# Attention, SoLU layer and Sinkhorn experts in one kernel: the first layer's input weights placed over the attention's memory, and the experts' first operands made beside the last units of the second matmul

## The chip, the cores and the metric

The kernel runs on one core of one Trainium2 chip. The metric is the device time of one execution in microseconds (us), lower is better. The program has five engines that work at once: TensorE (PE, matmuls), VectorE (DVE), ScalarE (ACT), GpSimd (POOL) and SyncE (SP, which here only issues DMAs). Each runs its own instructions in the order in which the program lists them.

## The reference, cut to what matters

```python
def reference(...):                       # q, k, v: (2, 8, 768, 64); 1536 tokens of 512 values in all
    # 1. attention with 4 sinks and a window of 128 keys
    scores = where(is_sink | in_window, q @ k.T / 8, -1e9)
    x = (softmax(scores) @ v)             # -> (1536, 512)
    # 2. SoLU layer
    h = x @ w_in                          # (1536, 1024)
    solu = h * softmax(h)
    ln = (solu - mean) / sqrt(var + 1e-6) * g_ln
    x = ln @ w_out                        # (1536, 512), called x2 below
    # 3. eight experts, weighed by a Sinkhorn matrix P (1536, 8) made from x @ w_gate in eight rounds
    for e in range(8):
        out += P[:, e:e+1] * (maximum(x @ w1[e], 0) @ w2[e])   # w1[e]: (512, 1024), w2[e]: (1024, 512)
```

## The kernel before, in words

Every matmul operand is split into a rounded part and a remainder ("hi" and "lo"), and a product is three matmuls, hi·hi, hi·lo and lo·hi (`mm3`, L82 to L88, whose three lines L83, L85 and L87 carry most matmuls of the trace).

*Attention and layer 2, tile by tile.* The 1536 tokens are 12 tiles of 128. A loop over slots s (eight heads a tile, 96 slots, and some more to drain) emits, for each slot, the scores of one head (`sc`), the softmax (`soft_exp`), transposes of the softmax of a pair of heads (`a_tr`, L494), the products with v (`av`, L522), and for each finished tile its normalisation and transposition (`x_tr`). Tile t then gets an "h unit" (`h_unit`): 24 matmuls into the PSUM tile hp, and behind it a chain of small steps: maximum (L235, DVE), exp (L238, ACT), product (L241, DVE), square (L249, ACT), power (L252, POOL), normalisation (L256, DVE), gains (L257, POOL), then transposes (L268, PE) and their split into `lt` (L67 ACT, L68 DVE). Each two tiles an "x2 unit" (`x2_unit`, 96 matmuls in two halves of 48, PSUM tile x2p) multiplies by w_out and puts the result into the four blocks x2f of 384 tokens. A half is copied out of PSUM by ACT (L310), or, where it straddles two blocks (x2 units 1 and 4), by ACT (L312) and DVE (L313). Units are numbered from 0: the last ones are h unit 11 and x2 units 4 (tiles 8 and 9) and 5 (tiles 10 and 11).

*The order.* Matmuls of h and x2 units wait in a queue, from which each slot takes 1.0 to 1.3 us worth (`bulk`). The small steps are emitted under `beside()`. A planner then orders each engine's instructions: of those that its own timing model calls ready, the one that stands first in the program. `tc.high_priority(offset=n)` counts an instruction as n places earlier; `beside()` has offset 0, the steps of an h unit's chain 60.

*Experts.* w1 is read in slices of 128 columns of each half (`load_w1`), combined by four sums (L684 to L687, POOL) into seven products' operands, and split by POOL (L76 rounds, L80 subtracts); w2 likewise without sums. The token side has seven operands for each half of the tokens, `build_x(n)`: sums and differences of x2f blocks (t1 to t4, L649) and "puts" (L644 ACT rounds, L645 DVE subtracts). `run` goes through 64 units (slice s, token half n): `first` is seven products of six matmuls (L716), with ReLU by ACT (L728) and its remainder by DVE (L729); `second`, of the unit before, is 36 matmuls and six accumulations. Slices 0 and 1 are made in `begin` (which follows the last x2 unit in the program) and `go_on`; build_x(0) stands in `begin`, build_x(1) as a whole ahead of unit 1. The logits and the Sinkhorn rounds are stepped beside the units (`step_side`).

*Memory.* Tiles live in pools that are opened and closed like a stack, from the left or the right. A tile laid over old ones waits until those that it overlaps have been read for the last time. Before, w_in and w_out share one pool that is closed after the last x2 unit; x0, wf (raw slices and temporaries) and w1a lie over the attention's pool; w1b, w2p and x1 over w_in and w_out.

## Time and profile before

| what | value |
|---|---|
| three runs, median | 1362.09 us (1361.94 to 1362.51) |
| profiled execution, its own time | 1362.57 us |
| its span, first to last instruction | 1360.5 us |
| PE busy | 1317.5 us, 97% |
| DVE, ACT, POOL busy | 708.2, 373.4, 541.9 us |
| mean granted PE clock | 0.982 of full speed |
| HBM traffic over the span | 41 GB/s |

All times in a trace are from the start of the span. The granted clock is given as a share of full speed: 1.00 is 2.4 GHz, 0.50 is 1.2 GHz. The attention and layer 2 take about the first 338 us, the experts the rest. Matmuls are pipelined, so their listed durations overlap.

### The profile page before, as it was taken

Reading aid. Unit: us, or ns where it says so; the run is one execution under the profiler, and the core shown is the slowest. Engines: PE = TensorE matmul, PEld = TensorE weight load, DVE = VectorE, ACT = ScalarE, POOL = GpSimd, SP = SyncE. Lnnn points to the kernel's source line nnn. Section 1 sums busy time; section 2 is a strip of 40 time slices with the busy share of each in tenths; the row PEclk is TensorE's granted clock in tenths of the full one; section 3 lists DMA queues with packets and bytes.
Section 4 is the critical chain, followed back from the end, with each engine's and each line's share of the span. In section 5 each row is a group of like instructions: output and inputs, shape, how many; then the busy total and the mean of one; then the engine's idle time right before and its main releaser. Section 6 shows DMA issues by size and latency. Waiting matters only on the chain.

```text
span 1360.5 us, 17867 instructions
## 1 busy us (share of the span) xinstructions
PE 1317.5 (97%) x6993; PEld 1171.5 (86%) x6993; DVE 708.2 (52%) x1352; ACT 373.4 (27%) x837; POOL 541.9 (40%) x560
## 2 busy tenths in 40 slices
PE   6799999987999999999999999999999999999998
PEld 5678888886789898989999999989999989999986
DVE  7976554544657454444444444544444544444544
ACT  5666454632422111111111111111111111111111
POOL 7862111243733643444333334444343333334410
PEclk9779999997999999999999999999999999999999
DMA  7411211001101111101111111111111001101102
GB/s 219 136 50 32 47 32 24 9 17 31 47 20 43 32 32 43 36 31 47 32 31 32 32 31 31 32 33 45 32 39 40 32 32 31 32 31 32 32 1 96
DMA packets 86287, 56.38 MB, mean 41 GB/s; under 512 B 41520, under 2 KB 74288, under 8 KB 86192
## 3 DMA queue, kind: packets, MB, share of 16 engines
q1 hardware_dynamic: 86192, 55.13, 13.8%
q8 instruction: 57, 0.93, 0.3%
q14 instruction: 38, 0.31, 0.1%
HBM read 51.97 MB, written 3.15 MB: 41 GB/s over the span
## 4 chain that ended last, share of the span: by engine, by line
PE 89%; DVE 4%; ACT 1%; issue 1%; POOL 0%; DVEq 0%; POOLq 0%; ACTq 0%
PE pb L716 15%; PE p L87 13%; PE p L85 13%; PE p L83 13%; PE pa L716 10%; PE pd L716 5%; PE pz L716 5%; PE av L522 2%; PE x2p L83 2%; PE x2p L85 2%; PE x2p L87 1%; PE hp L87 1%; PE hp L83 1%; PE hp L85 1%; DVE x L645 1%; PE trp L494 1%
## 5 line engine op out<-in xcount | busy, mean ns | idle before, releaser
L783 DVE SCALAR_TENSOR_TENSOR xa<-p,pr,xa 128x512 f32<-128x512 f32 x348 | 250.7, 748 | 207.0 <-PE p L87 207.0
L85 PE MATMUL p<-w,h 128*128 128x512 f32 x768 | 301.3, 392 | 0.0
L83 PE MATMUL p<-w,h 128*128 128x512 f32 x768 | 300.1, 391 | 0.5 <-DVE xa L783 0.5
L87 PE MATMUL p<-w,h 128*128 128x512 f32 x768 | 282.0, 394 | 2.1 <-DVE h L729 2.1
L716 PE MATMUL pb<-x,w 128*128 128x384 f32 x1152 | 234.0, 338 | 0.0
L76 POOL TENSOR_SCALAR w<-wf 128x1792 fp32r<-128x1792 f32 x32 | 54.3, 1697 | 437.2 <-PE pb L716 437.0
L716 PEld LDWEIGHTS pb<-x,w 128*128 128x128 f32 x1152 | 206.0, 188 | 5.7
L87 PEld LDWEIGHTS p<-w,h 128*128 128x128 f32 x768 | 143.6, 188 | 28.7 <-DVE h L729 2.5
L716 PE MATMUL pa<-x,w 128*128 128x384 f32 x768 | 167.1, 340 | 0.2 <-DVE h L729 0.2
L83 PEld LDWEIGHTS p<-w,h 128*128 128x128 f32 x768 | 144.2, 188 | 25.4 <-issue 0.9
L85 PEld LDWEIGHTS p<-w,h 128*128 128x128 f32 x768 | 144.2, 188 | 21.5
L728 ACT ACTIVATE h<-pz 128x384 fp32r<-128x384 f32 x64 | 31.4, 491 | 449.1 <-DVE pz L750 449.1
L716 PEld LDWEIGHTS pa<-x,w 128*128 128x128 f32 x768 | 139.2, 189 | 13.8 <-DVE h L729 0.5
L80 POOL TENSOR_TENSOR w<-wf,w 128x512 fp32r<-128x512 f32 (+1 forms) x128 | 148.3, 1191 | 2.6
L729 DVE SCALAR_TENSOR_TENSOR h<-pb,h 128x384 fp32r<-128x384 f32 x64 | 35.6, 557 | 159.5 <-ACT h L728 159.5
L80 POOL TENSOR_TENSOR w<-wr,w 128x512 fp32r<-128x512 f32 x64 | 83.7, 1330 | 0.2
L728 ACT ACTIVATE h<-pb 128x384 fp32r<-128x384 f32 x64 | 31.5, 492 | 179.1 <-PE pb L716 179.1
L716 PE MATMUL pz<-x,w 128*128 128x384 f32 x384 | 78.0, 338 | 0.0
L716 PE MATMUL pd<-x,w 128*128 128x384 f32 x384 | 77.9, 337 | 0.0
L750 DVE TENSOR_TENSOR pz<-pb,z 128x384 f32<-128x384 f32 x64 | 36.3, 566 | 76.6 <-PE pb L716 76.6
L716 PEld LDWEIGHTS pz<-x,w 128*128 128x128 f32 x384 | 69.2, 188 | 5.3
L83 PE MATMUL x2p<-lt,w 128*128 128x256 f32 x192 | 58.1, 303 | 10.1 <-DVE xa L313 8.9
(203 smaller groups left out, 1899.8 us busy)
## 6 DMA issues: line engine op xcount, KB each, us to landing
wf<-in_moe_w_dram SPq DMA_DIRECT2D x128, 128.0 KB, 2.3
wr<-in_moe_w_dram SPq DMA_DIRECT2D x32, 512.0 KB, 3.5
raw<-in_moe_w_in_dram SPq DMA_DIRECT2D x8, 512.0 KB, 5.9
raw<-in_moe_w_out_dram SPq DMA_DIRECT2D x8, 512.0 KB, 3.6
qk<-in_q_dram SPq DMA_DIRECT2D x12, 256.0 KB, 2.9
qk<-in_k_dram SPq DMA_DIRECT2D x12, 256.0 KB, 2.7
v<-in_v_dram SPq DMA_DIRECT2D x12, 256.0 KB, 2.8
out_dram<-xa SPq DMA_DIRECT2D x12, 256.0 KB, 3.5
```

The source lines that it names most:

```text
L76: nc.gpsimd.tensor_scalar(hi, src, 1.0, 0.0, ALU.mult, ALU.add)
L80: nc.gpsimd.tensor_tensor(lo[:, cs], src[:, cs], f32(hi[:, cs]), ALU.subtract)
L83: nc.tensor.matmul(ps, lhsT=lh, rhs=rh, start=start, stop=False)
L85: nc.tensor.matmul(ps, lhsT=lh, rhs=rl, start=False, stop=False)
L87: nc.tensor.matmul(ps, lhsT=ll, rhs=rh, start=False, stop=stop)
L494: nc.tensor.transpose(ps[:, hh, z], a[:, o:o + P], ident)
L522: nc.tensor.matmul(self.av_ps[:, h], lhsT=at[:, hh, z], rhs=self.raw["v", tv][:, h], start=h == 0 and n == 0, stop=h == H - 1 and n == len ...
L716: nc.tensor.matmul(ps, lhsT=a, rhs=b, start=start and kk == 0 and z == 0, stop=kk == 1 and z == 2, skip_group_check=True,)
L728: nc.scalar.activation(out=h[j][:, f, 0], in_=ps, func=ACTF.Relu)
L729: nc.vector.scalar_tensor_tensor(out=h[j][:, f, 1], in0=ps, scalar=0.0, in1=f32(h[j][:, f, 0]), op0=ALU.max, op1=ALU.subtract)
L750: nc.vector.tensor_tensor(out=pz, in0=pb, in1=z, op=ALU.add)
L783: nc.vector.scalar_tensor_tensor(out=acc, in0=ps, scalar=self.pr[:, t, e:e + 1], in1=acc, op0=ALU.mult, op1=ALU.add)
```

## The change

w_in gets a pool of its own in the attention's stack, so that it is released with the attention; w_out keeps its own. The experts' pools for raw slices (wfr), temporaries (wf), w2 (w2p) and both w1 buffers (w1a, w1b) open when h unit 11 has been emitted, over the attention and w_in. `build_x` makes seven tiles rather than one with seven parts, each put and difference in two halves, as a generator; `begin` is a generator too and is advanced two steps a slot beside x2 units 4 and 5; it now also splits slices 0 and 1 of w1 and w2. build_x(1) is advanced two steps at a time, twelve times over units 0 and 1. From slot 94 on `beside()` has offset 200. The attention's PSUM banks are released at slot 100, and give h unit 11 its own hp and the last x2 units a second x2p. x2's straddling halves are copied by ACT alone.

```diff
-    def w_slot():
-        n = w_count[0] % 8
-        w_count[0] += 1
-        return wpool.tile([P, 2, F], F32R, name=f"w{n}", tag=f"w{n}")
+    def w_slot(which, n):
+        return wpools[which].tile([P, 2, F], F32R, name=f"w_{which}{n}", tag=f"w_{which}{n}")
...
-    def x2_unit(p, pp):
+    def x2_unit(p, pp, tags=("mm", "mm")):
...
-            ps = pp["mm"].tile([P, 2, 2 * P], F32, name="x2p", tag="mm")
+            ps = pp[tags[d2]].tile([P, 2, 2 * P], F32, name="x2p", tag=tags[d2])
...
-                nc.vector.tensor_copy(x2f[t // 3 + 1][:, ds, 0:P], ps[:, :, P:])
+                nc.scalar.activation(out=x2f[t // 3 + 1][:, ds, 0:P], in_=ps[:, :, P:], func=ACTF.Copy)
...
         def open_early(self, stack):
+            self.wfr = pool(stack, "wfr", side="right")
+            self.wf = pool(stack, "wf", side="right")
+            self.w2p = pool(stack, "w2p", side="right")
+            w1b = pool(stack, "w1b", side="right")
             self.xp = [pool(stack, "x0", side="right")]
-            self.wf = pool(stack, "wf", side="right")
-            self.w1p = [pool(stack, "w1a", side="right")]
+            self.w1p = [pool(stack, "w1a", side="right"), w1b]
...
         def build_x(self, n, tp):
-            x = self.x[n] = self.xp[n].tile([P, 7, 2, 2, NX], F32R, name=f"x{n}")
+            x = self.x[n] = [None] * 7
+            for k in (self.X11, self.T3, self.T1, self.T2, self.X22, self.T4, self.X21):
+                x[k] = self.xp[n].tile([P, 2, 2, NX], F32R, name=f"x{n}_{k}", tag=f"x{n}_{k}")
...
             def put(k, src):
-                nc.scalar.activation(out=x[:, k, 0], in_=src, func=ACTF.Copy)
-                nc.vector.tensor_tensor(out=x[:, k, 1], in0=src, in1=f32(x[:, k, 0]), op=ALU.subtract)
+                for a in range(2):
+                    nc.scalar.activation(out=x[k][:, 0, a], in_=src[:, a], func=ACTF.Copy)
+                    nc.vector.tensor_tensor(
+                        out=x[k][:, 1, a], in0=src[:, a], in1=f32(x[k][:, 0, a]), op=ALU.subtract
+                    )
+                    yield
+            def minus(e, t, a, b):
+                for z in range(2):
+                    e.tensor_tensor(out=t[:, z], in0=a[:, z], in1=b[:, z], op=ALU.subtract)
+                    yield
+            t3, t1 = tp(0), tp(1)
+            yield from minus(nc.gpsimd, t3, b22, b12)
+            yield from put(self.X11, b11)
+            yield from minus(nc.vector, t1, b12, b11)
+            yield from put(self.T3, t3)
+            yield from put(self.X21, b21)
...
-            r = self.raw["1", s] = self.wf.tile([P, 8, 2, P], F32, name="wf", tag="wf")
+            r = self.raw["1", s] = self.wfr.tile([P, 8, 2, P], F32, name="wf", tag="wf")
...
+            build = self.build_x(1, lambda z: self.temp(("tt", "t1")[z]))
             for u, (s, n) in enumerate(units):
-                if u == 1:
-                    self.build_x(1, lambda z: self.temp(("tt", "h1")[z]))
-                if u < 2:
-                    step_side()
-                    step_side()
...
-                for _ in range(6):
+                for z in range(6):
                     next(a, None)
-                    if u > 1:
+                    if u > 1 or z in (1, 2) and not u:
                         step_side()
                     next(b, None)
+                    if u < 2:
+                        next(build, None)
+                        next(build, None)
...
         def begin(self):
-            self.build_x(0, lambda z: self.temp(("tt", "wr")[z]))
             self.load_w1(0)
+            build = self.build_x(0, lambda z: self.temp(("tt", "t1")[z]))
+            for _ in range(4):
+                next(build)
+                yield
             self.split_w1(0)
             self.load_w1(1)
-            self.load_w2(0)
-
-        def go_on(self):
-            for s in range(2):
-                self.split_w2(s)
-                self.load_w2(s + 1)
+            for z, _ in enumerate(build):
+                yield
+                if z == 5:
+                    self.load_w2(0)
+                    self.split_w2(0)
+                    self.load_w2(1)
             self.split_w1(1)
             self.load_w1(2)
+            yield
+            self.split_w2(1)
+            self.load_w2(2)
...
-            return tc.high_priority(offset=0)
+            return tc.high_priority(offset=0 if s < NS - 2 else 200)
...
-                    queue.insert(0, (s + 1, h_unit(tt, fast.x.pop(tt), pp, later, tr_q)))
+                    if tt == T - 1:
+                        psum_a.close()
+                        for nm in ("h", "mm"):
+                            pp[nm + "2"] = pool(psum_b, f"ps_{nm}2", space=PS)
+                    queue.insert(0, (s + 1, h_unit(tt, fast.x.pop(tt), pp, later, tr_q, "h2" if tt == T - 1 else "h")))
...
-            if att_open and s > NS + 6 and not queue:
-                att_open = False
+            if begin is None and s > LX + NS - H and not queue:
                 att.close()
                 ex.open_early(stack)
-                psum_a.close()
-                queue.append((s, x2_unit(T // 2 - 2, pp)))
-                queue.append((s + 10, x2_unit(T // 2 - 1, pp)))
-        ex.begin()
+                queue.append((s, x2_unit(T // 2 - 2, pp, ("mm2", "mm"))))
+                queue.append((s + 10, x2_unit(T // 2 - 1, pp, ("mm", "mm2"))))
+                begin = ex.begin()
+            if begin:
+                next(begin, None)
+                next(begin, None)
```

## Rows read from the trace of the kernel before

**Rows 1.** The page's heading: the span of the profiled execution.

```profile
span 1360.5 us, 17867 instructions
```

**Rows 2.** Windows, PE: stretch, its length, PE busy (matmuls), granted clock, DMA share, GB/s.

```profile
302.30:311.40 9.10, 0.26 (x3) 0.76 0.20 58
311.40:317.20 5.80, 5.78 (x27) 0.50 0.00 0
317.20:319.90 2.70, 2.70 (x23) 0.99 0.00 0
...
350.84:355.30 4.46, 4.46 (x16) 0.62 0.03 8
```

**Rows 3.** Timeline, PE: start, us, line, tiles; in brackets idle time before it, releaser.

```profile
311.42 0.58 PE L83 MATMUL x2p<-lt,w 128*128 128x256 f32 x1 [8.86 <-DVE xa L313]
...
322.43 1.09 PE L268 MATMUL trp<-ident,u 128*128 128x128 f32 x8 [2.47 <-POOL u L257]
...
350.84 0.50 PE L87 MATMUL p<-w,h 128*128 128x512 f32 x1 [2.12 <-DVE h L729]
```

**Rows 4.** Timelines of DVE and POOL, 301 to 325 us: tile 11's chain and what stands between.

```profile
301.13 1.23 DVE L235 TENSOR_REDUCE st<-hp 128x1 f32<-128x1024 f32 x1 [7.83 <-PE hp L87]
...
303.28 5.35 DVE L645 TENSOR_TENSOR x<-xa,x 128x768 fp32r<-128x768 f32 x3
...
309.75 1.21 DVE L241 CUSTOM_DVE_ANT_0 u<-hp,u 128x1024 f32<-128x1024 f32 x1
...
310.96 0.41 DVE L313 COPY xa<-x2p 128x256 f32<-128x256 f32 x1
...
323.75 1.29 DVE L68 TENSOR_TENSOR lt<-trp,lt 128x512 fp32r<-128x512 f32 x2 [2.92 <-ACT lt L67]
...
319.45 2.92 POOL L257 TENSOR_TENSOR u<-u,gains 128x1024 f32<-128x1024 f32 x1 [0.69 <-DVE u L256]
```

**Rows 5.** Timelines of DVE and POOL: first and last step of tile 10's chain.

```profile
283.10 1.22 DVE L235 TENSOR_REDUCE st<-hp 128x1 f32<-128x1024 f32 x1 [0.17 <-PE hp L87]
...
292.16 2.39 POOL L257 TENSOR_TENSOR u<-u,gains 128x1024 f32<-128x1024 f32 x1 [1.21 <-DVE u L256]
```

**Rows 6.** Timeline, ACT and PE: tile 11 from its last softmax to its h unit.

```profile
273.99 0.19 ACT L467 ACTIVATION_READ_ACCUMULATOR a<-a 128x1 f32 x1
...
280.85 0.27 PE L494 MATMUL trp<-ident,a 128*128 128x128 f32 x1
...
285.88 1.00 PE L522 MATMUL av<-v,at 128*128 128x64 f32 x8
...
294.85 0.39 PE L83 MATMUL hp<-w,xt 128*128 128x512 f32 x1
```

**Rows 7.** Timelines of SP and POOL: the first load, sums, rounding and subtraction of slices.

```profile
286.81 22.93 SPq L675 DMA_DIRECT2D wf<-in_moe_w_dram  x8
...
294.51 1.84 POOL L649 TENSOR_TENSOR tt<-xa 128x768 f32<-128x768 f32 x1
296.31 0.74 POOL L685 TENSOR_TENSOR wf<-wf 128x256 f32<-128x256 f32 x1
...
299.47 1.70 POOL L76 TENSOR_SCALAR w<-wf 128x1792 fp32r<-128x1792 f32 x1
301.25 6.56 POOL L80 TENSOR_TENSOR w<-wf,w 128x512 fp32r<-128x512 f32 x4
...
338.40 1.05 POOL L76 TENSOR_SCALAR w<-wr 128x1024 fp32r<-128x1024 f32 x1 [14.54 <-PE x2p L87]
...
394.08 4.49 POOL L80 TENSOR_TENSOR w<-wf,w 128x512 fp32r<-128x512 f32 x4
```

**Rows 8.** The chain that ended last: the same product 52 units apart (start, us, what).

```profile
518.33 1.06 PE pb L716 x6
...
1331.87 1.06 PE pb L716 x6
```

**Rows 9.** Timeline, DVE: a put alone, and three of build_x(1).

```profile
319.23 0.95 DVE L645 TENSOR_TENSOR x<-wr,x 128x768 fp32r<-128x768 f32 x1
...
341.84 6.54 DVE L645 TENSOR_TENSOR x<-xa,x 128x768 fp32r<-128x768 f32 x3
```

More of the change, by code (lines that the diff above doesn't have):

```diff
@@ L217, in drain, with h_unit @@
                 self.slot += 1
-    def h_unit(t, xt, pp, later, tr_q):
-        hp = pp["h"].tile([P, F], F32, name="hp", tag="h")
+    def h_unit(t, xt, pp, later, tr_q, tag="h"):
+        hp = pp[tag].tile([P, F], F32, name="hp", tag=tag)
         for kk in range(KD):
@@ L630, in open_rest @@
             self.xp.append(pool(stack, "x1"))
-            self.w1p.append(pool(stack, "w1b"))
-            self.w2p = pool(stack, "w2p")
             self.hp = pool(stack, "hp")
@@ L643, in put @@
             def put(k, src):
-                nc.scalar.activation(out=x[:, k, 0], in_=src, func=ACTF.Copy)
-                nc.vector.tensor_tensor(out=x[:, k, 1], in0=src, in1=f32(x[:, k, 0]), op=ALU.subtract)
-            def minus(e, z, a, b):
-                t = tp(z)
-                e.tensor_tensor(out=t, in0=a, in1=b, op=ALU.subtract)
-                return t
-            t3 = minus(nc.gpsimd, 0, b22, b12)
-            t1 = minus(nc.vector, 1, b12, b11)
-            put(self.X11, b11)
-            put(self.T3, t3)
-            put(self.X21, b21)
-            t2 = minus(nc.vector, 0, b22, t1)
-            put(self.T1, t1)
-            t4 = minus(nc.gpsimd, 1, b21, t2)
-            put(self.T2, t2)
-            put(self.T4, t4)
-            put(self.X22, b22)
+                for a in range(2):
[14 more added lines that the diff above has]
+            yield from put(self.X21, b21)
+            t2 = tp(0)
+            yield from minus(nc.vector, t2, b22, t1)
+            yield from put(self.T1, t1)
+            yield from put(self.T2, t2)
+            t4 = tp(1)
+            yield from minus(nc.gpsimd, t4, b21, t2)
+            yield from put(self.X22, b22)
+            yield from put(self.T4, t4)
         def temp(self, tag):
-            if tag == "h1":
-                return f32(self.hp.tile([P, 2, 2, NX], F32R, name="h1", tag="h1", bufs=2))[:, 0]
             return self.wf.tile([P, 2, NX], F32, name=tag, tag=tag)
@@ L793, in x_parts @@
             if b % 2 == 0:
-                return x[:, self.X11], x[:, self.X21]
+                return x[self.X11], x[self.X21]
             t = self.hp.tile([P, 2, 2, NX], F32R, name="h0", tag="h0", bufs=2)
@@ L1150, in general_path @@
         ex.open_early(stack)
-        ex.begin()
+        for _ in ex.begin():
+            pass
         ex.open_rest(stack)
```

28 lines of the change are left out of this document (15 added, 13 removed).

## The prediction

> **What bounds the kernel now.** I read the page first: the span is 1360.5 us [rows 1], and TensorE (PE) is busy almost all of it, so only stretches in which PE stands still or runs at the low clock can be won. The profiled execution took 1362.57 us, 2.07 us more than its span and 0.48 us more than the median of the runs shown.
>
> The PE windows of the stretch that the change touches come next [rows 2]. Until 302.3 PE is full. From 302.3 to 311.4 it works 0.26 of 9.10 us; then 27 matmuls take 5.80 us at a granted clock of 0.50 (1.2 GHz), where 23 matmuls of the same x2 unit take 2.70 us at 0.99, 0.117 us each. The reader is to see a long gap and, right behind it, half speed. From 350.84 to 355.3 the clock is low again (0.62), behind another wait.
>
> The PE timeline says who ended the waits [rows 3]: 8.86 us for the VectorE (DVE) copy that empties the first half of x2 unit 4 (L313), 2.47 us for GpSimd's (POOL) multiplication of tile 11 by the gains (L257), 2.12 us for DVE's ReLU remainder (L729). The queues behind it [rows 4]: as soon as tile 11's h unit ends, at 301.1, ScalarE (ACT) copies for build_x(0), and DVE takes three of its subtractions, 5.35 us. The product of tile 11 (L241), first in need, waits until 309.75, L313 until 310.96, and tile 11 has its gains only at 322.4. Tile 10 took 11.4 us for the same steps, from 283.10 to 294.55, with nothing of build_x beside it [rows 5].
>
> So the time to win: from 302.3 to the end of x2 unit 5 at 338.1 are 35.8 us, for 144 x2 matmuls (16.8 us at 0.117) and eight transposes (1.1 us, rows 3). **17.9 us are lost there.** Later, 2.1 us idle (rows 3), and 1.7 us of 4.46 (38% of full clock missing): **3.8 us.** The rest of the kernel is a row of equal units, 52 in 813.54 us, 15.645 us each [rows 8], which the diff doesn't touch.
>
> **The change, part by part.** *ACT empties x2 alone, and x2 units 4 and 5 alternate between two PSUM tiles.* The copy costs ACT about what it costs DVE; the second half of unit 4 no longer waits for any evacuation. The 8.86 us at 302.4 go. What is late next is tile 11: unit 5 needs its transposed normalisation.
>
> *Priority 200 from slot 94 on, and hp in a bank of its own for tile 11.* The program's order rules PE now: the last softmax piece is ready at 274.2, but its transposes, emitted at slot 96 after 18 matmuls of tile 10's h unit, begin at 280.85, 6.65 us later, and the last A·V products at 285.88; the h unit of tile 11 starts at 294.85 [rows 6] and ends at 301.1 (rows 4, L235 follows it). A lead of 200 instructions, some eight slots, puts these small steps ahead of h unit 10 and the x2 matmuls. From the transposes to h unit 11 lie some nine instructions, the longest 1.00 us (rows 6), so its input can be ready when PE ends h unit 10 at about 283.1 (rows 5: L235 follows it), and its own 24 matmuls, at most the 6.25 us that they took from 294.85 to 301.1, end at 289 at the earliest. If only the 6.65 us go, they end at 294.5. I take the first, because nothing on the way is long. PE's total work stays; x2 work moves behind. PE then has work until 302.3 + 5.6 (second half of unit 4) + about 0.4 = 308.3. Tile 11's chain needs 11.4 us and about 2 for transposes and evacuation, 13.4 in all as tile 10; beside build_x it took 23.9 (301.1 to 325.0, rows 4). From 289 the first gives 302.4, no gap, and from 294.5 still 307.9; the second from 289 gives 312.9, a gap of 4.6 and about 2.6 for the low clock behind it (5.80 us less 27 times 0.117). Neither excludes itself; half-size pieces, lead and a start before the stretch speak for the first. I take 1.5 us lost, and keep 0 and 7.2 for the range. **Gain 17.9 - 1.5 = 16.4.**
>
> *w_in over the attention's memory; w2p and w1b open early; raw slices in wfr.* At present w2(0) and w1(1) are rounded only after the last x2 matmul, behind a POOL wait of 14.54 us [rows 7], because their tiles lie over w_out. These now lie over w_in and the attention, free when tile 11's h unit ends. No time of its own on PE's path: its POOL work is covered by x2 units 4 and 5. That is four sums 0.74 each, 1.70 and four differences 4.49 for a w1 slice (9.15, twice), about 3.3 for a w2 slice (twice), 1.84 for each of t3 and t4, and the gains, 2.4: 31.0 in all (rows 5, 7; a w2 slice is 1.05 and two differences of 1.12). Without w2(1), needed only by unit 2, 27.7 must be done when unit 1 begins, about 322 + 7 products of 1.06 [rows 8] = 329. From 289 there are 40. If that cover is gone, unit 1 waits for what is left (the rival "operands late"). DMAs: SP's first slice of w1 was held until 286.81 by v's memory and should now go sooner; the others (four DMAs for w1(1), one each for w2(0) and w2(1), and those of slices 2 behind them) follow the POOL step that frees their tile, inside the same stretch.
>
> *Seven tiles per operand, built in halves.* Each tile waits only for what it lies over, so X11, X21 and X22 can be done while ACT and DVE stand idle before 301. A put alone takes 0.95 on DVE [rows 9]; in halves I charge the same (the bounds are nothing more, and a doubling, 6.7 us of DVE), hidden by PE's x2 work unless tile 11's chain pays, which the bound above holds.
>
> DVE's puts slow beside POOL: three in 5.35 us against 0.95 alone, while four of POOL's differences take 6.56 against 4.49 [rows 4, 7, 9]. Alone they make 7.3 us and together they took about 7.4 (301.2 to 308.6), so I count them as one after the other: 27.7 of POOL and 8.6 of DVE (seven puts, t1 and t2), 36.3 of the 40 us. The Trainium skill, SBUF — State Buffer, section "SBUF: two separate sides", says that the port pair which GpSimd shares with VectorE is an exclusive lock held for a whole instruction, also against a VectorE instruction with two SBUF inputs. By that rule the two sums add, as the rows here do; if they ran side by side only 27.7 would be needed. It is the rule that speaks against so much side work, and the rival "operands late" below is its case.
>
> *build_x(1) in 24 small steps over units 0 and 1.* Today the ReLU remainder stands behind 6.54 us and more of DVE puts (rows 9) and PE runs dry. With two half pieces a step it waits 1 to 2 us, for which logits and second-layer matmuls stand by. 8.6 us of DVE in the 23 us of two units fit. I take 1.0 of the 3.8 as kept (bounds 0 and 3.8). **Gain 2.8.**
>
> Sum: 1362.57 - 16.4 - 2.8 = 1343.4 for an execution like the profiled one, **1343** for a median run (0.48 less).
>
> **Rivals.**
> - *Tile 11 stays where it was* (22 in 100): the lead doesn't reach past h unit 10, or its inputs come too late in the planner's own timing. Then h ends near 301, the chain at 314.5 to 318, PE is out of work at 308: 6 to 10 us idle and 2.6 of low clock. Lost 9 to 13 rather than 1.5: 1350.5 to 1354.5, about 1352. For it: PE is full there and the order is computed, not measured. Against: the small steps wait there for their place in PE's order and for nothing else (rows 6).
> - *Operands late* (11 in 100): POOL and DVE work add up and POOL starts late or is caught behind a piece that waits for w_in; w1(1) is ready some 8 us after unit 1 wants it. 1351 (1347 to 1357). For it: 36 of 40 us are used. Against: the first slice can be split before tile 11's h unit ends, its memory being free by then.
> - *Slower* (6 in 100): POOL's queue keeps its order; if its side work of 28.6 us stands ahead of tile 11's gains, from 289 on, and DVE's 8.6 adds to it, the gains end at 328.6 and tile 11 is ready at 330. PE is then idle from 308, and with the low clock loses 24.4 us where it loses 17.9: 1366, the second gain taken off. It decides from about 329 on. Against: the gains have a lead of 200 and more, the side work none.
> - *Nothing* (5 in 100): the same with tile 11 ready near 327; the gap is filled no better than now: 1360 to 1364.
>
> **How the numbers follow.** The forecast has 56 in 100: 1343, its own range 1340 (nothing lost) to 1348 (most of the 7.2). About 0.2% (2.7 us) is what a measurement of this kernel can tell from no change. The first two rivals are faster as well: faster 0.89, same 0.05, slower 0.06. The range goes from 1338 (1362.1 - 17.9 - 3.8 = 1340.4, less 2 for short waits of the first units that I have not counted) to 1356, which takes in most of the first two rivals and leaves out about 2 in 10.
>
> **What would show it.** Right: no L313 on DVE; tile 11's first hp matmul before 290; the last x2 matmul near 322 with PE busy from 300 on and no clock of 0.50 there; rounding of w2(0) and w1(1) before that end; no PE wait over 1 us in units 0 and 1; 15.645 us a unit unchanged. Wrong: hp of tile 11 after 294, or a PE wait of more than 4 us for tile 11's transposes, for POOL's w or for DVE's x. If the first units wait for POOL or DVE more than they do today, the second gain was a loss.

## The result, and the profile after

The kernel after takes 1371.36 us (median of four runs, 1370.41 to 1372.11) beside 1362.24 us for the kernel before in the same session: 1.0066 times as long, 95% interval 1.0051 to 1.0081. It is slower by 9.1 us, where 1343 us was forecast, and lies outside the range. The profiled execution took 1370.41 us, its span is 1368.6 us. In the kernel after the lines have moved: the maximum L235 is L232, the product L241 is L238, the scaling L256 is L253, the gains L257 are L254, VectorE's puts L645 are L646, ScalarE's L644 are L645, the halves L649 are L653, the products L716 are L721.

The span is split below at four instructions that both traces have (times of their starts): the last matmul of tile 11's h unit, the last x2 matmul, and the two products of [rows 8], which now start at 522.37 and 1339.81.

| stretch | before | after | difference |
|---|---|---|---|
| start to the last h matmul | 300.70 | 296.75 | -3.95 |
| to the last x2 matmul | 37.33 | 44.48 | +7.15 |
| to the first of the two products | 180.30 | 181.14 | +0.84 |
| 52 units | 813.54 | 817.44 | +3.90 |
| to the end of the span | 28.68 | 28.81 | +0.13 |
| sum | 1360.55 | 1368.62 | +8.07 |

Of the first row, 1.92 us are not the change's: the last softmax already ended at 272.26 instead of 274.18, and kernels with the same code there as before reached the last h matmul between 299.7 and 303.3 in other executions. Two losses are to be explained: 7.15 us between tile 11's h unit and the end of x2, and 3.90 us (0.075 us each) in units that the diff doesn't touch.

PE in windows of the kernel after (columns as in [rows 2]):

```profile
302.30:305.80 3.50, 3.50 (x30) 1.00 0.00 0
305.80:325.89 20.09, 0.01 (x2) 0.56 0.17 52
325.89:333.00 7.11, 7.11 (x35) 0.57 0.25 76
333.00:341.50 8.50, 8.50 (x72) 1.00 0.21 63
346.50:351.20 4.70, 3.27 (x16) 1.00 0.00 0
```

and its PE timeline, the rows with a wait:

```profile
325.89 1.97 PE L265 MATMUL trp<-ident,u 128*128 128x128 f32 x8 [20.09 <-POOL u L254]
...
347.09 1.31 PE L721 MATMUL pa<-x,w 128*128 128x384 f32 x6 [1.76 <-ACT pb L746]
...
350.29 0.50 PE L83 MATMUL p<-w,h 128*128 128x512 f32 x1 [0.84 <-ACT h L733]
```

The wait of 8.86 us for VectorE's copy [rows 3] is gone, as forecast, and PE does all of x2 unit 4 by 305.8. Then it has nothing to do until tile 11 has its gains: one wait of 20.09 us in place of 8.86 and 2.47, and 35 matmuls at a granted clock of 0.57 behind it. The wait of 2.12 us for the ReLU remainder has become two, 1.76 and 0.84 us, for ScalarE; the window from 346.50 shows no low clock between them.

VectorE and GpSimd of the kernel after from the end of tile 11's h unit on, in two timelines (answering [rows 4]):

```profile
297.18 1.23 DVE L232 TENSOR_REDUCE st<-hp 128x1 f32<-128x1024 f32 x1 [5.19 <-PE hp L87]
298.32 3.26 DVE L653 TENSOR_TENSOR t<-xa,xa 128x384 f32<-128x384 f32 x2
301.50 8.59 DVE L646 TENSOR_TENSOR x<-xa,x 128x384 fp32r<-128x384 f32 x6
310.02 1.61 DVE L646 TENSOR_TENSOR x<-tt,x 128x384 fp32r<-128x384 f32 x1
311.55 1.21 DVE L238 CUSTOM_DVE_ANT_0 u<-hp,u 128x1024 f32<-128x1024 f32 x1
...
313.36 0.54 DVE L646 TENSOR_TENSOR x<-t,x 128x384 fp32r<-128x384 f32 x1
...
321.46 1.50 DVE L253 TENSOR_SCALAR u<-u,st 128x1024 f32<-128x1024 f32 x1
```

```profile
297.22 1.99 POOL L653 TENSOR_TENSOR tt<-xa 128x384 f32<-128x384 f32 x2 [2.68 <-PE hp L87]
299.16 2.02 POOL L76 TENSOR_SCALAR w<-wf 128x1792 fp32r<-128x1792 f32 x1
...
302.47 5.68 POOL L80 TENSOR_TENSOR w<-wf,w 128x512 fp32r<-128x512 f32 x4
308.11 3.10 POOL L80 TENSOR_TENSOR w<-wr,w 128x512 fp32r<-128x512 f32 x2
...
323.50 2.33 POOL L254 TENSOR_TENSOR u<-u,gains 128x1024 f32<-128x1024 f32 x1
```

Read them side by side. The maximum of tile 11 is done at 298.4, its exponential ran on ScalarE from 299.26 and was read out at 300.45, but the product, which needs nothing else, starts at 311.55: nine pieces of build_x(0) stand between the two in VectorE's queue, and while GpSimd works beside them they take 1.5 us each. At 313.36 GpSimd stands idle and the same piece takes 0.54 us. In the kernel before, t1 as a whole and three whole puts stand in this place, as much as eight of these pieces. t1 goes ahead of the puts of [rows 4]:

```profile
302.27 1.08 DVE L649 TENSOR_TENSOR wr<-xa,xa 128x768 f32<-128x768 f32 x1
```

There they take 6.4 us (302.27 to 308.63), here the nine take 13.3 (298.32 to 311.63). From the maximum to the end of the gains are 28.7 us, to VectorE's last copy of the transposes 32.0 us, where [rows 5] has 11.4 and the prediction allowed 23.9 at most.

Tile 11's way to its h unit (ACT and PE of the kernel after, answering [rows 6]):

```profile
272.07 0.19 ACT L464 ACTIVATION_READ_ACCUMULATOR a<-a 128x1 f32 x1
...
275.23 0.27 PE L491 MATMUL trp<-ident,a 128*128 128x128 f32 x1
...
281.37 0.27 PE L499 MATMUL trs<-ident,sa 128*96 128x128 f32 x1
281.68 0.27 ACT L503 ACTIVATE as<-trs 96x128 fp32r<-96x128 f32 x1 [4.72 <-PE trs L499]
...
287.41 0.60 PE L321 MATMUL trp<-ident,xs 128*128 128x128 f32 x4
```

The lead did move the softmax's transposes, from 6.65 us behind the last softmax to 2.97; but the sinks' transposition came only at 281.37, and the last A·V products of the softmax with it (281.91), though ScalarE had copied their input by 276.95. PE had matmuls of tile 10's h unit ahead of both. The h unit ended 24.92 us behind the last softmax (297.18 less 272.26), before 26.95 (301.13 less 274.18).

The steady units, by the window 520 to 1330 us, in which PE is busy throughout in both kernels. First the kernel before (length, busy and matmuls, clock, DMA share, GB/s), then the kernel after:

```profile
520.00:1330.00 810.00, 810.00 (x4041) 1.00 0.10 32
```

```profile
520.00:1330.00 810.00, 810.00 (x4021) 1.00 0.11 33
```

At the same granted clock of 1.00 the kernel after has 20 matmuls fewer in the same 810 us. No wait is listed there; the matmuls themselves come more slowly.

### The profile page after: what moved, and what is told of

Read it like the earlier page. It is cut to its first block, busy times and chain, and to the rows that moved or that the text cites. A ratio compares the mean times of both kernels' runs of the same rounds, so it can differ in the third digit from the quotient of the medians.

```text
span 1368.6 us, 17901 instructions
## 1 busy us (share of the span) xinstructions
PE 1318.7 (96%) x6993; PEld 1169.0 (85%) x6993; DVE 710.6 (52%) x1366; ACT 376.0 (27%) x855; POOL 537.3 (39%) x564
## 3 DMA queue, kind: packets, MB, share of 16 engines
q1 hardware_dynamic: 86192, 55.13, 13.7%
## 4 chain that ended last, share of the span: by engine, by line
PE 89%; DVE 4%; ACT 1%; POOL 1%; issue 1%; DVEq 0%; ACTq 0%; POOLq 0%
PE pb L721 15%; PE p L83 13%; PE p L85 13%; PE p L87 13%; PE pa L721 10%; PE pd L721 5%; PE pz L721 5%; PE av L519 2%; PE x2p L85 2%; PE x2p L83 2%; PE x2p L87 2%; PE hp L87 1%; PE hp L85 1%; PE hp L83 1%; DVE x L646 1%; PE trp L491 1%
## 5 line engine op out<-in xcount | busy, mean ns | idle before, releaser
L721 PE MATMUL pb<-x,w 128*128 128x384 f32 x1152 | 233.2, 337 | 0.0
L721 PEld LDWEIGHTS pb<-x,w 128*128 128x128 f32 x1152 | 204.9, 188 | 5.4
L721 PE MATMUL pa<-x,w 128*128 128x384 f32 x768 | 166.6, 338 | 3.0 <-ACT pb L746 2.8
L721 PEld LDWEIGHTS pa<-x,w 128*128 128x128 f32 x768 | 139.1, 188 | 17.5 <-ACT pb L746 3.5
L80 POOL TENSOR_TENSOR w<-wf,w 128x512 fp32r<-128x512 f32 (+1 forms) x128 | 145.1, 1167 | 2.4
L721 PE MATMUL pz<-x,w 128*128 128x384 f32 x384 | 78.8, 339 | 0.0
L721 PE MATMUL pd<-x,w 128*128 128x384 f32 x384 | 78.4, 336 | 0.0
L721 PEld LDWEIGHTS pz<-x,w 128*128 128x128 f32 x384 | 69.6, 188 | 5.3
L721 PEld LDWEIGHTS pd<-x,w 128*128 128x128 f32 x384 | 67.9, 188 | 0.2
```

What stands on the lines that cost most here:

```text
L80: nc.gpsimd.tensor_tensor(lo[:, cs], src[:, cs], f32(hi[:, cs]), ALU.subtract)
L721: nc.tensor.matmul(ps, lhsT=a, rhs=b, start=start and kk == 0 and z == 0, stop=kk == 1 and z == 2, skip_group_check=True,)
```

## The experiments

Ratios are to the kernel before on the same chip, with their 95% intervals; the median of before was 1362.67 us in the first session, 1362.48, 1361.31 and 1362.46 us in the others.

**e1: ScalarE alone empties x2, in the kernel before.**

```diff
-                nc.vector.tensor_copy(x2f[t // 3 + 1][:, ds, 0:P], ps[:, :, P:])
+                nc.scalar.activation(out=x2f[t // 3 + 1][:, ds, 0:P], in_=ps[:, :, P:], func=ACTF.Copy)
```

> The kernel before with one edit alone: the half tile of x2 that VectorE copied out of PSUM is copied by ScalarE. Theory A (the chain of tile 11's gains on VectorE and GpSimd sets the end of the first x2 units, so who copies x2 out is off that path): 1362.2 us, no change beyond 1 us either way. Rival (the evacuation itself held TensorE between tiles 10 and 11): 1359 us or less, and the wait of 8.86 us on VectorE's xa is shorter by 3 us or more.

1361.67 us, 0.9993 (0.9984 to 1.0003): no change. PE's waits in this run:

```profile
305.99 0.39 PE L83 MATMUL x2p<-lt,w 128*128 128x256 f32 x1 [3.60 <-ACT xa L313]
...
321.89 1.97 PE L268 MATMUL trp<-ident,u 128*128 128x128 f32 x8 [9.94 <-POOL u L257]
```

The first wait is shorter by 5.3 us, as the rival had it, and the next one longer by 7.5. The copy was in the way, but tile 11's chain stands right behind it: removing one wait alone buys nothing.

**e2: w2 moved by 1,920 bytes, in the kernel before.** A pool of 1,920 bytes is opened ahead of w2's and one of 128 bytes behind it; nothing uses them.

```diff
+            pool(stack, "pad0").tile([P, 480], F32, name="pad0")
             self.w2p = pool(stack, "w2p")
+            pool(stack, "pad1").tile([P, 32], F32, name="pad1")
```

> The kernel before with two pads that move the two tiles of w2 in SBUF by 1,920 bytes and leave everything else where it was; nothing is computed otherwise. Theory A (the second layer's matmuls of 512 columns are slower in the kernel after because of the address at which w2 lies): the steady units take 15.72 us instead of 15.645, matmuls of 512 columns start every 231.7 ns instead of 229.6, and the time is 1367 us (plus 4 to 5). Rival (the rate goes by something else in the kernel after, such as the banks of PSUM or the order of the engines): units stay at 15.645 us and the time at 1362.2, within 0.7.

1367.56 us, 1.0037 (1.0023 to 1.0051). In PE's window:

```profile
520.00:1330.00 810.00, 810.00 (x4021) 1.00 0.11 33
```

4021 matmuls, as in the kernel after; a unit takes 15.72 us. The two pads also move what lies behind w2, by 2,048 bytes together; e17 shows that such a move alone costs nothing. So the address of w2 alone makes the steady units as slow as there.

**e3: w1(0) rounded first, in the kernel after.** In `begin`, `split_w1(0)` and `load_w1(1)` go ahead of the first four pieces of build_x(0).

```diff
-            for _ in range(4):
-                next(build)
-                yield
             self.split_w1(0)
             self.load_w1(1)
-            for z, _ in enumerate(build):
+            for z, _ in enumerate(build, -4):
```

> The kernel after, with the sums and the rounding of the first expert's w1 and the load of the second's moved ahead of the work on x0, so that GpSimd does not have them to do beside tile 11's gains. Theory A (GpSimd's side work beside tile 11's chain makes VectorE's puts and halves two to three times as long, and delays GpSimd's own steps of the chain): VectorE's six puts take near 0.5 to 0.7 us each instead of 1.43, the product of tile 11's chain starts at 304 to 307 us instead of 311.6, the gap of 20 us on TensorE shrinks by 5 to 8, and the time is 1363 to 1367 us. Rival (VectorE's and ScalarE's own queue order sets the chain, GpSimd is no part of it): the gap stays within 2 us of 20, the time within 1 us of 1371.4.

1371.70 us, 1.0066 (1.0052 to 1.0079), wait of PE 20.96 us. GpSimd's timeline says why it tells little:

```profile
295.51 1.70 POOL L76 TENSOR_SCALAR w<-wf 128x1792 fp32r<-128x1792 f32 x1
298.22 1.99 POOL L653 TENSOR_TENSOR tt<-xa 128x384 f32<-128x384 f32 x2 [1.01 <-PE hp L87]
300.15 5.79 POOL L80 TENSOR_TENSOR w<-wf,w 128x512 fp32r<-128x512 f32 x4
```

Only the rounding moved ahead of t3; the four differences still run beside VectorE's puts. The edit didn't make the case that it was meant to make.

**e4: no lead of 200, in the kernel after.**

```diff
-            return tc.high_priority(offset=0 if s < NS - 2 else 200)
+            return tc.high_priority(offset=0)
```

> The kernel after, with the experts' first work at the priority of before beside the last attention units (no lead of 200). Theory A (the lead is what moves the first product of tile 11 ahead but leaves the h unit where it was): h unit 11 ends within 2 us of 297 us, and the time is 1370 to 1373. Rival (the lead puts the puts and halves ahead of tile 11's product on VectorE, and without it they stand behind it): the product starts before 302 us, the gap on TensorE is under 14 us, and the time is 1364 us or less.

1372.39 us, 1.0073 (1.0058 to 1.0087), wait 20.49 us. The h unit ended at 302.97, later than either theory had it; 3.8 us of that are a softmax that ended later in this execution (276.04). Behind the softmax it is 26.93 us, as in the kernel before: the lead is worth 2.0 us on that way. The pieces on VectorE stand between maximum and product without it too.

**e5: the temporaries over q, k and v, in the kernel after.** The seven operand tiles also lie in the order in which they are made.

```diff
-            self.wf = pool(stack, "wf", side="right")
             self.w2p = pool(stack, "w2p", side="right")
             w1b = pool(stack, "w1b", side="right")
             self.xp = [pool(stack, "x0", side="right")]
+            self.wf = pool(stack, "wf", side="right")
...
-            for k in (self.X11, self.T3, self.T1, self.T2, self.X22, self.T4, self.X21):
+            for k in (self.X11, self.T3, self.X21, self.T1, self.T2, self.X22, self.T4):
```

> The kernel after with the pools on the right opened in another order, so that build_x(0)'s two temporaries lie over q, k and v (free some 20 us before tile 11's h unit ends) and not over w_in, and the seven operand tiles lie in the order in which they are made; nothing is computed otherwise. Theory A (the temporaries lie over w_in, so the halves and puts of build_x(0) wait for tile 11's h unit and then stand on VectorE between the first and the third step of tile 11's chain): t1 and most puts are done before tile 11's h unit ends at 297 us, the product of tile 11's chain starts before 304 us instead of 311.6, the wait of 20 us on TensorE shrinks to 8 to 13, and the time is 1360 to 1365 us. Rival (the order was fixed by the recorded priorities, not by the memory): the puts stay behind 297 us, the wait stays within 2 us of 20, the time within 1.5 us of 1371.

1369.04 us, 1.0050 (1.0035 to 1.0066), wait 17.77 us. t3 started at 295.01 on GpSimd, ahead of the end of the h unit, but VectorE's order stayed: the maximum first, then t1 and the puts. Memory was one thing that held the pieces back; their place in VectorE's queue was the other, and it decided.

**e6: w1(0)'s and w2(0)'s rounding written behind build_x(0), in the kernel after.**

```diff
-            self.split_w1(0)
-            self.load_w1(1)
+            self.load_w2(0)
             for z, _ in enumerate(build):
                 yield
-                if z == 5:
-                    self.load_w2(0)
-                    self.split_w2(0)
-                    self.load_w2(1)
+            self.split_w1(0)
+            self.load_w1(1)
+            self.split_w2(0)
+            self.load_w2(1)
             self.split_w1(1)
```

> The kernel after with all sums, rounding and differences of w1(0) and w2(0) moved behind the whole of build_x(0), so GpSimd has only t3 and t4 beside tile 11's chain. Theory A (GpSimd's differences of 1.4 us each stretch VectorE's puts, and both share one port): the six puts in a row take 0.5 to 0.7 us each instead of 1.43, the product of the chain starts at 303 to 306 us, the wait of 20 us on TensorE is shorter by 5 to 8; the first expert's units may then wait for w1 or w2, up to 8 us. Rival (VectorE's puts in halves cost 1.4 us by themselves): no put gets shorter than 1.2, the wait on TensorE stays.

1371.45 us, 1.0067 (1.0052 to 1.0081), wait 20.09 us. GpSimd's order in the trace came out as in the kernel after (t3, the two roundings, six differences, from 300.11 to 314.1). Where a piece is written in `begin` did not set its place in the queue, so the run tells nothing of contention.

**e7: w2 back on the left at a multiple of 2,048 bytes, rounded behind x2, in the kernel after.** `split_w2(0)` and `split_w2(1)` go from `begin` back to `go_on`, as in the kernel before.

```diff
         def open_early(self, stack):
-            self.w2p = pool(stack, "w2p", side="right")
...
         def open_rest(self, stack):
+            self.w2p = pool(stack, "w2p")
             self.xp.append(pool(stack, "x1"))
```

> The kernel after with w2's two tiles back on the left side at a multiple of 2,048 bytes, opened behind x2 as in the kernel before, and their rounding behind the last x2 unit again. Theory A (the slower steady units come from the address of w2 alone): units take 15.645 us instead of 15.72, and 1371.4 goes to 1366 to 1367 us, more only if the first second-layer matmuls wait for w2(0). Rival (something else in the kernel after slows the units too, such as its other banks of PSUM): units stay above 15.69 us.

1368.79 us, 1.0052 (1.0035 to 1.0068). The window 520 to 1330 has 4031 matmuls, a unit 15.677 us: half of the loss is back, not all. Where the rest lies can be read from the starts of the matmuls. The second-layer matmuls start 229.3 ns apart again where they follow each other, as in the kernel before (231.8 in the kernel after). Products of the first layer, whose moving operand is x, are slower than before: those into `pa` start 178.0 ns apart instead of 176.8.

And PE's wait fell to 16.51 us though only GpSimd's work on w2 had left the stretch. VectorE of this run:

```profile
302.42 6.71 DVE L646 TENSOR_TENSOR x<-xa,x 128x384 fp32r<-128x384 f32 x6
309.05 0.55 DVE L646 TENSOR_TENSOR x<-tt,x 128x384 fp32r<-128x384 f32 x1
309.52 1.21 DVE L238 CUSTOM_DVE_ANT_0 u<-hp,u 128x1024 f32<-128x1024 f32 x1
```

GpSimd's last difference ended at 307.8 here instead of 311.2; the seven puts took 7.2 us instead of 10.1. This is the test that e3 and e6 were meant to be: take 4.5 us of GpSimd's work out of the stretch, and VectorE's puts get 2.9 us shorter.

**e10: w2's even slices 1,024 bytes and its odd ones 128 bytes past a multiple of 2,048, in the kernel before.** The tile of slice s is taken from `self.w2p[s % 2]`.

```diff
-            self.w2p = pool(stack, "w2p")
+            pool(stack, "pad0").tile([P, 256], F32, name="pad0")
+            w2a = pool(stack, "w2a")
+            pool(stack, "pad1").tile([P, 288], F32, name="pad1")
+            self.w2p = [w2a, pool(stack, "w2b")]
+            pool(stack, "pad2").tile([P, 480], F32, name="pad2")
```

> The kernel before with w2's tile of the even slices 1,024 bytes past a multiple of 2,048 and that of the odd slices 128 bytes past one; nothing is computed otherwise. Theory A (the rate suffers when a row of 512 columns, 2,048 bytes, starts off a multiple of 2,048 bytes, however far off): both kinds of unit take 15.72 us, the time is 1367 us. Rival (only small steps count, such as whether the start is a multiple of 1,024 bytes): the even slices take 15.645 and the odd ones 15.72, the time is 1364.7 us.

1364.77 us, 1.0015 (1.0006 to 1.0024), 4030 matmuls in the window, 15.68 us a unit. Which slices pay shows where 18 second-layer matmuls follow each other with no product between. Counted through, 36 a unit and two units a slice, these are the first and the last of 18 of slice 30, and then of slice 31, the last one:

```profile
1324.55 0.40 PE L83 MATMUL p<-w,h 128*128 128x512 f32 x1
...
1328.42 0.39 PE L87 MATMUL p<-w,h 128*128 128x512 f32 x1
...
1340.21 0.40 PE L83 MATMUL p<-w,h 128*128 128x512 f32 x1
...
1344.18 0.39 PE L87 MATMUL p<-w,h 128*128 128x512 f32 x1
```

From first to last are 3.87 us for the even slice, as in the kernel before (1322.36 to 1326.23), and 3.97 us for the odd one, where the kernel before has 3.90 (1338.01 to 1341.91). From 525 to 1320 us the matmuls of even slices start 228.9 ns apart on the mean, as before, those of odd slices 232.6 instead of 229.7. So the rival was right, in its time too: 128 bytes cost, 1,024 don't.

**e16 and e17: w2 at 512 and 256 bytes past a multiple, and moved by exactly 2,048 bytes, in the kernel before.** e16 is e10 with pads of 128, 448 and 448 elements, e17 has one pad of 512 elements ahead of w2's pool.

> The kernel before with w2's tile of the even slices 512 bytes past a multiple of 2,048 and that of the odd slices 256 bytes past one; nothing is computed otherwise. Theory A (small offsets cost nothing, large ones do; 128 bytes were free, 1,024 cost 0.066 us a unit): at least the odd slices (256) stay at the times of before, the even ones cost 0 to 0.07 us a unit; time 1362 to 1365 us. Rival (128 bytes were free by chance of something else, such as which tiles VectorE writes meanwhile): both cost 0.07 us a unit, 1367 us.

> The kernel before with w2 and all that lies behind it on the left moved by exactly 2,048 bytes; nothing is computed otherwise. Theory A (what counts is the address modulo 2,048 bytes): units stay at 15.645 us and the time within 0.7 us of before. Rival (any move of w2 changes the rate, by its place among larger blocks): units differ by 0.03 us or more, the time by 2 us or more.

1362.46 us, 0.9999 (0.9990 to 1.0008), and 1362.02 us, 0.9997 (0.9988 to 1.0006). Both have 4041 matmuls in the window and 15.645 us a unit. The expectation of e16 starts from a wrong reading of e10, in which the two kinds of slices are the other way round; its theory A had the result right, but not for its reason. In these tries a start 0, 256, 512 or 1,024 bytes past a multiple of 2,048 is free, and one 128 (e10) or 1,920 (e2) past it costs about 0.07 us a unit of 36 second-layer matmuls. The free distances are multiples of 256 bytes, the two that cost are not; whether that is the rule was not tried further.

**e11: everything of `begin` queued behind tile 11's own steps, in the kernel after.** `tail` holds tile 11's square on ScalarE, its scaling on VectorE and its gains on GpSimd; what is traced inside the block is queued behind them, each on its engine. The first load of w1 goes ahead of it.

```diff
...
+        def behind():
+            es = ExitStack()
+            for ins in pp["tail"]:
+                es.enter_context(tc.issue_after(ins))
+            return es
...
-            if begin:
-                next(begin, None)
-                next(begin, None)
+            if begin and "tail" in pp:
+                with behind():
+                    next(begin, None)
+                    next(begin, None)
...
```

> The kernel after with all of build_x(0), the rounding of w1(0), w1(1) and w2 held, on each engine's queue, behind tile 11's own steps (ScalarE's square, VectorE's scaling, GpSimd's gains); nothing else moves, w2 stays where it lies. Theory A (the side work that stands between the steps of tile 11 on VectorE and GpSimd is what made its chain 32 us long): the chain takes 11 to 14 us, the wait of 20 us on TensorE goes down to 4 to 7; the first expert's operands are then late by up to 8 us behind the last x2 unit; the time is 1360 to 1368 us, steady units stay at 15.72. Rival (the chain is long by its own steps, PSUM or the low clock): chain above 20 us, time within 2 us of 1371.

1365.91 us, 1.0037 (1.0023 to 1.0050), units still at 15.72. From the maximum to the end of the gains are 11.7 us instead of 28.7, to VectorE's last copy of the transposes 22.6 instead of 32.0. In place of 20.09 us PE waits 3.12 us for the gains, 0.76 us for ScalarE's copy of the transposes and 5.88 us for VectorE's; then 5.24 us in the first two units for the ReLU remainder.

**e13: the same, with w2 as in e7 and w1(0) rounded ahead of tile 11's chain.**

```diff
...
+                with tc.high_priority(offset=400):
+                    ex.load_w1(0)
+                    ex.split_w1(0)
+                    ex.load_w1(1)
                 begin = ex.begin()
...
```

> The same with w2 on the left side at a multiple of 2,048 bytes, opened behind x2, and w1(0) rounded ahead of tile 11's chain, in the time in which GpSimd stood idle. Theory A: wait on TensorE 4 to 7 us before x2 unit 5, no wait over 2 us for w1(0), units at 15.68 us, time 1350 to 1357 us, faster than both kernels. Rival (the operands made late cost as much as the chain gains): another wait of 8 us or more ahead of unit 0, time 1360 or more.

1365.30 us, 1.0037 (1.0023 to 1.0051). x2 ends at 332.2 instead of 341.2, but the first units lose it again:

```profile
338.37 1.34 PE L724 MATMUL pa<-x,w 128*128 128x384 f32 x6 [2.12 <-ACT pb L749]
...
346.26 0.50 PE L87 MATMUL p<-w,h 128*128 128x512 f32 x1 [3.43 <-DVE h L737]
```

My forecast of 1350 to 1357 was wrong. Twelve pieces of build_x(1) stand on VectorE between the end of x2 and the first ReLU remainder, where the kernel after has thirteen; but GpSimd now has w2 to round beside them, and they take 12.1 us instead of 7.8.

**e14: e13, and build_x(1)'s pieces queued behind the copies and ReLUs that stand ahead of them in the program.** `self.act` and `self.dve` hold the last copy or ReLU of the unit on ScalarE and VectorE.

```diff
...
                     if u < 2:
-                        next(build, None)
-                        next(build, None)
+                        with ExitStack() as es:
+                            for ins in (self.act, self.dve):
+                                if ins is not None:
+                                    es.enter_context(tc.issue_after(ins))
+                            next(build, None)
+                            next(build, None)
...
```

> The same as e13 with the pieces of build_x(1) queued behind those copies and ReLUs of the first two units on ScalarE and VectorE which stand ahead of them in the program. Theory A (the waits of 1.8 and 2.5 us in the first two units come from pieces of build_x(1) that stand ahead of unit 0's copies on ScalarE): both waits fall below 0.7 us, the time is 2 to 4 us less than e13's. Rival (those waits have another cause, or come back in unit 2, where build_x(1)'s last tiles are needed): within 1 us of e13's time.

1355.82 us, 0.9959 (0.9945 to 0.9972): faster than both kernels, and 9.5 us below e13 where 2 to 4 were expected. Of the waits in units 0 and 1 one of 0.86 us is left. What still stands on PE ahead of them, with VectorE's rows that end it:

```profile
309.97 1.97 PE L268 MATMUL trp<-ident,u 128*128 128x128 f32 x8 [2.65 <-POOL u L255]
...
319.96 0.58 PE L85 MATMUL x2p<-lt,w_out 128*128 128x256 f32 x1 [5.19 <-DVE lt L68]
```

```profile
316.81 2.49 DVE L649 TENSOR_TENSOR x<-t,x 128x384 fp32r<-128x384 f32 x2
319.23 0.68 DVE L68 TENSOR_TENSOR lt<-trp,lt 128x512 fp32r<-128x512 f32 x1
```

**e15: e14, with `tail` on ScalarE and VectorE moved on to the last copies of tile 11's transposes.** `split_psum` returns its two instructions; the gains stay in `tail`.

```diff
...
-                split_psum(lt[:, 0, fs, t % 2], lt[:, 1, fs, t % 2], ps)
+                two = split_psum(lt[:, 0, fs, t % 2], lt[:, 1, fs, t % 2], ps)
+                if t == T - 1 and g == 1:
+                    pp["tail"] = tail + two
...
```

> The same as e14 with the work on x0 held, on ScalarE and VectorE, behind the copies of tile 11's transposes out of PSUM and not only behind the square and the scaling. Theory A (the 5.19 us for which TensorE still waits are puts that stand ahead of VectorE's copy of the transposes): that wait falls to 1 us or less, the last x2 matmul goes from 332.5 to 327 us or so, the time is 1350 to 1353 us. Rival (the 5 us come back as late operands of unit 0 or unit 1): another wait of 3 us or more behind the last x2 matmul, time within 1.5 us of 1355.8.

1354.11 us, 0.9940 (0.9927 to 0.9954), the lowest of all, though its interval overlaps that of e14. Its chain (VectorE, then GpSimd) and PE's waits:

```profile
298.60 1.23 DVE L234 TENSOR_REDUCE st<-hp 128x1 f32<-128x1024 f32 x1 [5.19 <-PE hp L88]
301.16 1.23 DVE L240 CUSTOM_DVE_ANT_0 u<-hp,u 128x1024 f32<-128x1024 f32 x1 [1.33 <-ACT u L237]
...
311.02 1.29 DVE L68 TENSOR_TENSOR lt<-trp,lt 128x512 fp32r<-128x512 f32 x2 [3.86 <-ACT lt L67]
```

```profile
307.30 2.34 POOL L256 TENSOR_TENSOR u<-u,gains 128x1024 f32<-128x1024 f32 x1 [1.19 <-PE x2p L88]
```

```profile
309.70 1.12 PE L267 MATMUL trp<-ident,u 128*128 128x128 f32 x8 [2.46 <-POOL u L256]
311.04 0.80 PE L84 MATMUL x2p<-lt,w_out 128*128 128x256 f32 x2 [0.22 <-ACT lt L67]
...
336.25 0.49 PE L86 MATMUL p<-w,h 128*128 128x512 f32 x1 [3.11 <-POOL w L81]
```

From the maximum to the end of the gains are 11.0 us, to the last copy 13.7. x2 ends at 325.4. Part of the 7 us that this wins over e14 goes into a wait of 3.11 us for w2(0), which now stands late in GpSimd's queue (and 0.98 us for ScalarE): the rival of this run was right in part, and the time lies 1 us above the range that I gave.

## Why the prediction was wrong

*That ScalarE's copy and two PSUM tiles take the 8.86 us away* was right, and so was *what is late next is tile 11*. e1 shows both in the kernel before: with the copy on ScalarE alone the first wait falls to 3.60 us, and the wait for tile 11 grows to 9.94.

*"So its input can be ready when PE ends h unit 10 ... end at 289 at the earliest"* failed. The h unit ended at 297.1, 24.9 us behind the last softmax. The lead won 2.0 us (e4), not 12, and these 2.0 are no gain by themselves: PE's x2 work moved behind the h unit by as much. I followed the transposes and products of the softmax alone. The sinks' transposition, which tile 11 also needs, was not in my list, and ScalarE waited 4.72 us for it; and the last A·V products, which were in it, kept their place behind tile 10's h unit too. The rival "Tile 11 stays where it was" was right here. By itself it would have given 1352 us.

*"Beside build_x it took 23.9 ... I take 1.5 us lost"* is the step that cost most. I took the 23.9 us that the kernel before needs beside build_x as the upper bound; the chain took 32.0. By size the side work between the maximum and the product hardly grew (nine halves for eight); what grew is its price, since t3, both roundings and six differences of GpSimd now ran beside it, where [rows 4] and [rows 7] have four differences. A bound read from a row with less of GpSimd's work beside it did not hold. Of the 8.1 us over 23.9 this stretch has 5.8, and 1.5 more lie between the product and the scaling. PE lost 20.09 us of waiting, and 2.8 at the low clock (7.11 us for eight transposes of 1.1 us in all and 27 x2 matmuls of 0.117), 22.9 instead of 17.9. With the h unit's end at 297.18 and the end of x2 unit 4 at 305.8, a chain of 13.4 us would have left a gap of 4.8; e15 has the chain at 13.7 and PE waiting 2.7 us. So the length of the chain is shown to be the loss, and its cause is the side work between its steps: e11 and e15 move that work, and nothing of the chain's own.

*"In halves I charge the same"* was about right for a piece alone (two of 0.54 us for 0.95) and wrong beside GpSimd. The seven puts from 301.50 and the six differences from 302.47 would alone take 3.8 and 6.7 us (0.54 and 1.12 each, [rows 7]), 10.5 in all; together they took 10.1 (301.50 to 311.63). The single records take turns, one for one: differences end at 304.05, 305.61 and 307.15, puts at 304.46, 306.03 and 307.57. So a half lets as much of GpSimd's work pass as a whole put does: it takes 1.6 us in such a turn, where the first two whole puts of [rows 4] take 2.0 each. No run put whole pieces in the same place. The Trainium skill, SBUF — State Buffer, section "SBUF: two separate sides", says that the pair of ports that GpSimd and VectorE share is held for a whole instruction, and the other blocked. This trace agrees but for 0.4 us: 3.8 and 6.7 make 10.5, beside 10.1 measured. (The prediction's own reading, 7.3 us alone for 7.4 together, leaves out t1's 1.08 us in the same stretch; with it 8.4 us of work took 7.4, so a part ran side by side there.) I had used that sum for the question whether the operands come in time, and not for the chain, whose steps stand in the same queues.

*"Against: the gains have a lead of 200 and more, the side work none"* (the rival "Slower"). Tile 11's gains did stand ahead of some of the later side work; but a lead helps only a step whose input is there. The pieces were taken in the gap between two steps of the chain, short as planned, long as executed, and a queue that has begun them gives nothing back. That rival had GpSimd's queue as its place. Here the first and larger delay was on VectorE, between the maximum and the product; tile 11 was ready at 329.2, which was the point from which I said it decides, and the 22.9 us lost are near the 24.4 that I gave it.

*"The first slice can be split before tile 11's h unit ends"*: its sums were, at 97.6 us already; its rounding stood behind t3 in GpSimd's queue, and t3 waited for the memory of w_in (2.68 us, released by the last h matmul). The memory that the change reuses comes free when tile 11's chain begins, and so all that waits for it starts at the same moment as the chain. e5 moved the temporaries and took 2.3 us off PE's wait.

*"Operands late"* did not happen in the kernel after, since tile 11 was later still. It appears in e15, as 3.11 us.

*build_x(1) in small steps, gain 2.8*: from the last x2 matmul to the product eleven units on took 181.14 us instead of 180.30, and eleven slower units account for 0.8. The gain was nothing. The wait went from VectorE's queue to ScalarE's, where nine puts stood ahead of unit 0's first copy. e14 shows it: with the pieces in the program's order no wait for ScalarE or VectorE is left in units 0 and 1, only 0.86 us for GpSimd.

*"15.645 us a unit unchanged"* failed. By the program's layout, which no trace shows, w2's tiles moved from a multiple of 2,048 bytes to 1,920 past one; e2 gives the loss by that alone, and e7 half of it back. In e7 (and in e13 to e15, 4031 or 4032 matmuls) the second layer is as fast as before; what is left of the loss shows in first-layer products, and in the units of the second token half, 15.736 us instead of 15.672. The moving operand x of these products lies elsewhere than in the kernel before; what the addresses of x, w1 and h do to the rate was not tried, so this cause stays open.

Sum in the terms of the prediction: instead of 16.4 us gained, 5.0 lost (22.9 for 17.9); instead of 2.8, nothing; and 4.7 in the units (63 by 0.075), a term that I had at nothing. That makes 9.7 us slower, beside 9.1 measured. In the two profiled spans, 8.07 apart, the 1.92 us by which the attention happened to end earlier come off: 7.8.

## What to carry to other kernels

Work that fills the gaps of a chain runs at the price that it has beside its neighbours, not at its price alone; where two engines take turns, count the filled gap with both engines' sums, and don't bound it by a row in which the other engine had less to do. Cutting a piece in halves gives the other engine more turns within it. Memory that comes free at the moment at which a critical chain starts releases everything at once, into the same queues: order that work behind the chain by hand. Priorities and the place in the program moved little here (e3, e4, e6); an explicit order of the queues (e11, e14, e15) is what gave the change its gain.

## What the runs showed of the hardware that was not expected

The rate of matmuls depended on where in SBUF their moving operand lies. In otherwise equal kernels w2's rows of 512 columns, with both tiles at a multiple of 2,048 bytes, gave 4041 matmuls in 810 us (before; e17, moved by exactly 2,048), and as many at 512 and 256 past one (e16); both tiles at 1,920 past gave 4021 (e2). With one tile at 1,024 and the other at 128 past it were 4030 (e10), and the second alone was slower: 232.6 ns from start to start where the kernel before has 229.7. e2 has 232.3 ns for 229.3. All this is at a granted clock of 1.00 and with no wait listed. Other distances, and with what such reads collide, were not tried.
